# A planned attention and two-layer kernel on one core: new constants and a longer search for the plan's order

## The chip, the cores and the metric

The kernel runs on one core of one Trainium2 chip, in one launch. The time is the device time of one execution in microseconds (us). Smaller is better. Before the change three executions took 516.48, 516.94 and 519.18 us; their median is 516.94 us.

The engines are named as the profile names them: PE is TensorE, PEld its loading of weights, DVE is VectorE, ACT is ScalarE, POOL is GpSimd, SP is SyncE, which here only issues transfers.

## The reference

There are 4 sequences of 576 rows and 512 columns. Three layers follow one another; all arithmetic is asked for to the accuracy of 32-bit floats, and the weights come as 64-bit floats.

```python
# 1. attention: 8 heads of 64 columns; heads 0-3 see the last 32 positions,
#    heads 4-7 see earlier positions with the same remainder modulo 32
scores = scale * q @ k.T;  scores = where(mask, scores, -1e9)
x = softmax(scores) @ v
# 2. channel mix: x_prev is x moved down by one row
xk = mu_k * x + (1 - mu_k) * x_prev;  xr = mu_r * x + (1 - mu_r) * x_prev
x = sigmoid(xr @ w_r) * (relu(xk @ w_k) ** 2 @ w_v)      # 512 -> 1024 -> 512
# 3. gated layer: a convolution over three rows makes the gate
h = relu(x @ w_in)                                        # 512 -> 1024
out = (h * sigmoid(conv3(h, conv_w))) @ w_out             # 1024 -> 512
```

## The kernel before

Each 32-bit operand of a large product is split into a high and a low part, and a product is three matrix multiplications (high by high, low by high, high by low), of 288 or 512 columns each.

The work of the core has two stages, each with a plan of its own.

**First stage: attention and the channel mix.** Attention of a sequence is 8 units (4 pairs of heads, 2 halves each). A unit has scores on PE (`sc`, line 560), a mask and a row maximum on DVE (`masked`, line 576), exponentials on ACT (`exps`, line 581), a division on DVE (line 592), a transposition on PE (`tr`, lines 604 and 614) that ACT or DVE copies out (`pt`), the product with the values on PE (`pv`, lines 637 and 646), and a copy out into `xT`. The channel mix works on chunks of half a sequence (288 columns). `mix` makes `mx`, then its high and low parts: set `Y` for w_r, set `X` for w_k (lines 734 to 737; the high parts on ACT, the low parts on DVE). `Y00` to `Y31` and `X00` to `X31` are four blocks of 128 rows each, high (second digit 0) and low (second digit 1). Weights come in pieces: a transfer of the raw 64-bit words (`raw`), three instructions that make 32-bit words (`narrow`: `wb` at line 386, `wt` at 393, 394 and 397), and two that split them (`wrh` and `wrl`, `wkh` and `wkl`, `wvh` and `wvl`, lines 436 and 437). The products of the channel mix (`mm`) are all at line 755. For sequence 0 come 96 matmuls with w_r (eight groups of 12) and 192 with w_k, whose groups need all of `X`, then those with w_v. The other sequences follow; their attention is laid between the products.

**Second stage: the gated layer.** Products with w_in (`hh`, line 1010; 16 pairs of blocks of 42 matmuls each, four pairs to a sequence), a chain of DVE and ACT instructions for each of two blocks in a pair (`hb`, `c`, lines 1018 to 1059), its split (`gA`, `gB`, lines 1063 and 1064), and the products with w_out (`oo`, line 1078; 18 groups of 24 matmuls).

**What sets the order.** The code of the two stages adds jobs to a `Plan`: a job has its engines with a cost on each, a function that issues its instructions, what it reads and writes, and the number of bytes of a transfer. `Plan.run` goes through the jobs as if in time: it takes the job that can start earliest on its engine by the plan's costs (of those that start together the one with the highest rank), and puts it next on that engine. Jobs with two engines (mostly copies) go to the one that is earlier. The instructions are issued in exactly the order that comes out. The plan knows buffers (a `Space` has a tag and a number of buffers; a new one waits until an old one is released), the time of transfers (`DMA_RATE`, in bytes per us, `DMA_LATENCY`), the loading of a table on ACT (1.29 us where the table changes), and a model of how PE gets its instructions (`CHUNK`, `AHEAD`, `FETCH`, `CROWD`). Where PE would idle for longer than 0.48 us early in the first stage, the kernel puts matmuls without use on it (`stir`, line 922, from a tile of zeros named `idle`; 10 more stand at the start, into `scrap`): the number is the planned idle time less 0.3 us, divided by 0.17 us.

`search` repeats `run` with ranks changed at random by `vary`, from a list of seeds in `STEPS`: each seed changes the ranks that the seed before left. Only seeds that were kept when the list was made stand in it: 39 for the first stage and 30 for the second.

Of the kernel before, what the change touches and what calls it, by code (L numbers as in the profile page):

```python
# [2 lines left out]

# [24 lines left out]
BANKS = {"sc": 2, "tr": 2, "pv": 1, "mm": 3}  # L28
WARM, MIXES, BEHIND = 10, 2, (0, 3)
REBIAS = 2.0 ** -112  # L30
DMA_RATE, DMA_LATENCY = 280.0e3, 2.0
FOREVER = 1.0e9
PREFER, PREFER_FROM, BESIDE = 0.5, 20.0, 0.3
QUEUE, FEED = 64, 0.0142
CHUNK, AHEAD, FETCH, CROWD = 256, 85, 4.0, (0.3, 7.0)
GAP = {("mm", "half"): 0.09, ("tr", "half"): 0.17, ("tr", "tr"): 0.08}
ENTER = {("half", "mm"): 0.11, ("tr", "mm"): 0.085, ("half", "tr"): 0.05}
STEPS = (
    (
# [4 lines left out]
    ),  # L44
    (
# [3 lines left out]
    ),  # L49
)  # L50
HALF_ARRAY = {"sc", "pv"}
BLOCKS = ("B11", "B21", "B22", "T4", "T1", "T2", "T3")
WEIGHTS = ("A11", "A12", "A22", "S3", "S4", "S1", "S2")
# [4 lines left out]
SCRATCH = 1024  # L58
TAIL = 20.0
LQ, LK, LW, LB, LEAD = 64, 64, 96, (5, 4), 3  # L60
STIR_UNTIL = 60.0
BANKED = {"sc", "tr", "pv", "mm"}
RIGHT = {"raw", "ws", "wt", "wb", "qk", "vt", "pr", "nmx", "sums", "rec", "pt"}
LATENCY = {"PE": 0.22, "ACT": 0.16, "DVE": 0.12, "POOL": 0.12, "SP": 0.0}
# [27 lines left out]
class Plan:  # L92
# [89 lines left out]

    def vary(self, seed, keep, at, end):

        draw, tried = random.Random(seed), list(keep)
        t0, width = draw.uniform(0.0, end), draw.choice((8.0, 25.0, 400.0))
        amount, share = draw.choice((0.3, 1.0, 3.0)), draw.choice((0.05, 0.3))
        for i, j in enumerate(self.jobs):
            if abs(at[i] - t0) <= width / 2 and draw.random() < share:
                rank, lean = tried[i]  # L190
                if len(j.engines) > 1 and draw.random() < 0.5:
                    lean = draw.uniform(-0.6, 0.4)
                tried[i] = rank + draw.gauss(0.0, amount), lean
        return tried

    def search(self, start=None, steps=()):
# [26 lines left out]
    def run(self, start=None, limit=None):  # L223

        free = dict(start or dict.fromkeys(LATENCY, 0.0))
        dma, table, out, kind, filled, fetched, usable, leave = 0.0, None, [], "mm", 0.0, AHEAD, 0.0, 0.0
        wait = {j: len(j.before) for j in self.jobs}
        at = {j: [] for j in self.jobs}
        ready = {e: [] for e in LATENCY}
        left, todo = len(self.jobs), sum(j.engines.get("PE", 0.0) for j in self.jobs)  # L230

        def release(j):
            for e in j.engines:
                t = max([end + (ITSELF if by == e else LATENCY).get(by, 0.0) for end, by in at[j]], default=0.0)
                ready[e].append((t, j))

        for j in self.jobs:
            tags = {s.tag for s in j.spaces}
            j.kind = "half" if ("sc" in tags or "vt" in tags) else "tr" if "tr" in tags else "mm"
            if not wait[j]:  # L240
                release(j)
        while left:
            best, bound = None, FOREVER
            for e, jobs in ready.items():
                now = free[e]
                for t, j in jobs:
                    if t < now:
                        t = now
                    if t > bound + 1.0:
                        continue  # L250
                    for s in j.spaces:
                        if not s.open:
                            t = max(t, self.slot(s, j))
                    if t > bound + 1.0:
                        continue
                    late = t
                    if e == "DVE" and len(j.engines) > 1:
                        late += j.lean + PREFER * (t > PREFER_FROM)
                    if e == "PE":
                        late += max(0.0, self.feed(j, t, filled, fetched, usable, dma)[0] - t - j.engines[e])  # L260
                        late -= BESIDE * (kind == j.kind == "half")
                    key = (round(late, 2), -j.rank, j.n)
                    if t < FOREVER and (best is None or key < best[0]):
                        best, bound = (key, t, e, j), late
            assert best, "no job can start"
            _, t, e, j = best
            if e == "PE":
                t = max(t, free[e] + (GAP.get((kind, j.kind), 0.0) if kind != "half" else leave * (j.kind != "half")))
                idle = t - free[e]
                if self.stirred and 5.0 < t < STIR_UNTIL and idle > 0.48 and self.room(j, free[e]):  # L270
                    j.room, j.idle = self.room(j, free[e]), int((idle - 0.3) / 0.17)
                    fetched += 2 * j.idle
                    if fetched % CHUNK < 2 * j.idle:
                        usable = t + FETCH + CROWD[0] * min(CROWD[1], max(0.0, dma - t))
                else:
                    j.room = None
            for s in j.spaces:
                if not s.open:
                    s.open = True
                    self.opened[s.tag] += 1  # L280
            cost = j.engines[e]
            if e == "PE":
                cost += ENTER.get((kind, j.kind), 0.0)
                filled, fetched, usable = self.feed(j, t, filled, fetched, usable, dma)
                cost = max(cost, filled - t)
                kind, leave = j.kind, j.leave
                todo -= j.engines[e]
                if limit is not None and t + cost + todo > limit:
                    return None
            if j.table and j.table != table:  # L290
                cost += 1.29
                table = j.table
            if j.nbytes:
                free[e] = t + cost
                dma = max(dma, t + DMA_LATENCY) + j.nbytes / DMA_RATE
                j.end = dma
            else:
                free[e] = j.end = t + cost
            for k in j.engines:
                ready[k] = [x for x in ready[k] if x[1] is not j]  # L300
            for s in j.spaces:
                s.left -= 1
                s.end = max(s.end, j.end + LATENCY[e] * (not j.nbytes))
            for k in j.after:
                at[k].append((j.end, None if j.nbytes else e))
                wait[k] -= 1
                if not wait[k]:
                    release(k)
            out.append((j, e, t, j.end))
            j.done = True  # L310
            left -= 1
        return out
# [3 lines left out]
def block_kernel(ctx, tc, qkL, qkS, vL, vW, vS, mu_k, mu_r, w_k, w_v, w_r, w_in, conv_w, w_out, ident, mask_l, mask_w, mask_s, out):  # L316
# [603 lines left out]
    def stir(n, into, anew=True):  # L920
        for _ in range(n):
            pe.matmul(into[:, :T], idle[:, :P], idle, start=anew, stop=anew)
# [40 lines left out]
    def issue(stirred=False):  # L963
        plan.stirred = stirred
        with tc.manual_schedule():
            if stirred:
                stir(WARM, scrap)
            for job, e, start, end in plan.search(START if stirred else SECOND, STEPS[not stirred]):
                if e == "PE":
# [237 lines left out]
```

## Time and profile before

| | |
|---|---|
| three executions | 516.48, 516.94, 519.18 us |
| the profiled execution | 519.4 us, of which the trace's span is 517.6 us |
| PE busy | 508.3 us (98% of the span), 4886 matmuls |
| weight loads (PEld) busy | 472.0 us (91%) |
| DVE busy | 386.7 us (75%), 1142 instructions |
| ACT busy | 352.0 us (68%), 1075 instructions |
| DMA | 90.27 MB, mean 174 GB/s |
| chain that ended last, by engine | PE 85%, ACT 9%, DMA 3%, DVE 3%, issue 1% |
| granted clock of PE, mean | 0.998 |

All times in the views are us from the start of the span. A busy PE is not PE at work on the reference: the matmuls of `stir` count as busy too. Stages are found by the names: `mm` alone ends the first stage, and the first long run of `hh` begins the second.

### The profile page before, as it was taken

The numbers are of one execution on the slowest core, as the hardware profiler recorded it, in microseconds if no ns is written. First come the engines' busy times: TensorE is split into PE (matmuls) and PEld (weight loads), VectorE is DVE, ScalarE is ACT, GpSimd is POOL, SyncE is SP. The second block draws the span as 40 slices with busy tenths as digits, with TensorE's granted clock in tenths as the row PEclk, the third lists the DMA queues.
The fourth block names the chain that finished last, engine by engine and source line by source line (L and its number), as shares of the span: only waits on it lengthen the run. The fifth ranks groups of instructions, "written<-read, shape, count | busy, mean of one in ns | idle before, by whom it ended". The sixth has DMA issues, their size and how long they took to land.

```text
span 517.6 us, 12872 instructions
## 1 busy us (share of the span) xinstructions
PE 508.3 (98%) x4886; PEld 472.0 (91%) x4886; DVE 386.7 (75%) x1142; ACT 352.0 (68%) x1075; POOL 1.6 (0%) x15
## 2 busy tenths in 40 slices
PE   8989999999999999999999999999999999999997
PEld 5679999899999899999999999999998898988885
DVE  3999999898957988868877415699984697970910
ACT  5999996899758999857799243466663465542520
POOL 0000000000000000000000000000000000000000
PEclk9999999999999999999999999999999999999999
DMA  8956664884385982597683730854162163110111
GB/s 291 325 186 210 209 201 159 293 272 155 132 277 187 312 294 96 194 321 206 240 304 120 226 104 2 304 203 140 47 222 76 57 204 152 47 41 27 36 41 61
DMA packets 50653, 90.27 MB, mean 174 GB/s; under 512 B 4256, under 2 KB 32672, under 8 KB 50592
## 3 DMA queue, kind: packets, MB, share of 16 engines
q1 hardware_dynamic: 50304, 89.29, 51.5%
q8 instruction: 38, 0.62, 0.5%
q14 instruction: 23, 0.19, 0.1%
q10 hardware_dynamic: 288, 0.16, 0.1%
HBM read 60.80 MB, written 28.64 MB: 173 GB/s over the span
## 4 chain that ended last, share of the span: by engine, by line
PE 85%; ACT 9%; DMA 3%; DVE 3%; issue 1%; ACTq 0%; DVEq 0%
PE mm L755 43%; PE oo L1078 19%; PE hh L1010 17%; ACT pr L581 3%; PE sc L560 2%; PE pv L646 2%; PE tr L614 1%; DMA raw<-in_w_in 1%; ACT mx L734 1%; ACT wb L386 1%; DMA wi_d<-ws 1%; DMA qk<-in_qkL 1%; ACT Y L736 1%; DVE pr L576 1%; DVE pr L592 0%
## 5 line engine op out<-in xcount | busy, mean ns | idle before, releaser
L1010 PEld LDWEIGHTS hh<-x,wi 128*128 128x128 f32 x672 | 91.9, 188 | 2.1 <-DVE x L819 0.3
L1010 PE MATMUL hh<-x,wi 128*128 128x288 f32 x672 | 93.4, 296 | 0.1
L755 PE MATMUL mm<-X,wvh 128*128 128x288 f32 x448 | 83.9, 298 | 0.0
L755 PE MATMUL mm<-Y,wkh 128*128 128x288 f32 x384 | 68.1, 295 | 0.0
L755 PEld LDWEIGHTS mm<-X,wvh 128*128 128x128 f32 x448 | 66.9, 188 | 0.3
L581 ACT ACTIVATE pr<-pr,nmx 128x54 f32<-128x54 f32 (+2 forms) x160 | 53.8, 347 | 4.9 <-DVE nmx L576 4.8
L755 PEld LDWEIGHTS mm<-Y,wkh 128*128 128x128 f32 x384 | 56.4, 188 | 0.0
L755 PE MATMUL mm<-Y,wrh 128*128 128x288 f32 x256 | 56.0, 300 | 0.3 <-ACT rs L767 0.2
L1057 DVE SCALAR_TENSOR_TENSOR c<-hb,cw_sb,c 128x576 f32<-128x576 f32 x64 | 50.2, 812 | 0.4
L755 PE MATMUL mm<-X,wvl 128*128 128x288 f32 x224 | 47.9, 295 | 0.0
L755 PEld LDWEIGHTS mm<-Y,wrh 128*128 128x128 f32 x256 | 42.2, 188 | 1.5 <-ACT rs L767 0.4
L1078 PE MATMUL oo<-wo,gAh 128*128 128x512 f32 x160 | 43.2, 391 | 0.0
L755 PE MATMUL mm<-Y,wkl 128*128 128x288 f32 x192 | 40.9, 294 | 0.0
L755 PE MATMUL mm<-Y,wrl 128*128 128x288 f32 x128 | 38.1, 297 | 0.8 <-DVE wrl L437 0.7
L1088 ACT ACTIVATE ob<-oo 128x512 f32<-128x512 f32 x17 | 10.0, 597 | 38.5 <-PE oo L1078 38.1
L755 PEld LDWEIGHTS mm<-X,wvl 128*128 128x128 f32 x224 | 35.9, 188 | 0.0
L1078 PE MATMUL oo<-wo,gBh 128*128 128x512 f32 x128 | 34.4, 390 | 0.0
L1078 PEld LDWEIGHTS oo<-wo,gAh 128*128 128x128 f32 x160 | 29.1, 188 | 5.2
L1058 ACT ACTIVATE c<-c 128x576 f32<-128x576 f32 x32 | 21.8, 683 | 16.6 <-DVE c L1057 16.4
L581 ACT ACTIVATION_READ_ACCUMULATOR pr<-pr,nmx 128x1 f32 x160 | 32.2, 201 | 0.0
L778 ACT ACTIVATE rl<-mm 128x288 f32<-128x288 f32 x64 | 25.6, 406 | 9.3 <-PE mm L755 9.2
L796 DVE TENSOR_TENSOR X<-sq,X 128x288 fp32r<-128x288 f32 x48 | 21.7, 456 | 13.6 <-ACT X L794 11.8
(123 smaller groups left out, 1072.4 us busy)
## 6 DMA issues: line engine op xcount, KB each, us to landing
x_d<-xo SPq DMA_DIRECT2D x42, 288.0 KB, 3.0
x<-x_d SPq DMA_DIRECT2D x21, 576.0 KB, 4.7
wi_d<-ws SPq DMA_DIRECT2D x24, 256.0 KB, 3.4
wi<-wi_d SPq DMA_DIRECT2D x6, 896.0 KB, 6.2
qk<-in_qkS SPq DMA_DIRECT2D x8, 599.0 KB, 5.5
out<-ob SPq DMA_DIRECT2D x18, 256.0 KB, 2.0
qk<-in_qkL SPq DMA_DIRECT2D x7, 592.0 KB, 4.9
raw<-in_w_k SPq DMA_DIRECT2D x8, 512.0 KB, 3.9
```

What stands on the lines that cost most here:

```text
L386: act.activation(b(), hw, AF.Copy, scale=REBIAS)
L560: pe.matmul(bank_of[j]()[to + u:to + u + m, at_[j]:at_[j] + nk], qk()[r, qo[j] + u:qo[j] + u + m], qk()[r, ko[j] + u:ko[j] + u + nk], star ...
L581: act.activation(pr()[:, k], pr()[:, k], AF.Exp, bias=nmx()[:, i:i + 1], scale=-1.0, accum_out=sums()[:, i:i + 1])
L646: pe.matmul(outs_[odd]()[r, i * nq + u:i * nq + u + m], vt()[part, v, r], pt()[part, o:o + m], start=True, stop=True)
L755: pe.matmul(o(), w_cols(name, j, t, part), x_[t](), start=(t == 0 and part == 0 and x_ is xhi), stop=(t == nk - 1 and x_ is xlo))
L778: plan.add({"ACT": 0.295}, lambda e: act.activation(r(), o(), AF.Relu), [o], [r])
L796: plan.add({"DVE": 0.37}, lambda e: dve.tensor_tensor(l_(), sq(), h_().bitcast(F32), ALU.subtract), [sq, h_], [l_])
L1010: pe.matmul(o(), w(hw, j), x()[:, hx, j], start=anew and n == 0 and j == 0, stop=last and n == 2 and j == 1, skip_group_check=True)
L1057: plan.add({"DVE": 0.735}, lambda e, k=k: dve.scalar_tensor_tensor(c(), h()[:, k:k + S], cw_sb[:, k * NF + f:k * NF + f + 1], c(), ALU.mul ...
L1058: plan.add({"ACT": 0.6}, lambda e: act.activation(c(), c(), AF.Sigmoid), [c], [c], table="sigmoid")
L1078: pe.matmul(o(), x_()[:, f, col:col + P], wsp["wo", f]()[:, part], start=(f == 0 and x_ is th and part == 0), stop=(f == NF - 1 and x_ is tl))
L1088: act.activation(ob(), o(), AF.Copy, scale=0.5)
```

## The change

Three things change; the instructions of a job, its operands and its dependencies do not.

- Constants of the plan: `DMA_RATE` 280 to 365 (thousand bytes per us), `FETCH` 4.0 to 4.4 and `CROWD` (0.3, 7.0) to (0.4, 6.0) in the model of PE's instruction fetch; the plan starts with the exponential's table loaded instead of none; a PE job of the first stage that starts before 6.0 us counts 1.7 times; and an idle PE before 7.0 us gets one `stir` matmul for each 0.26 us instead of each 0.17 us.
- `vary` draws its numbers by its own arithmetic instead of the library's, and has a second kind of change: with a chance of 0.4 it shifts the ranks of 4 to 120 neighbouring jobs together.
- `STEPS` holds 61 seeds for the first stage and 43 for the second. The key of a job is rounded in another way.

```diff
-DMA_RATE, DMA_LATENCY = 280.0e3, 2.0
+DMA_RATE, DMA_LATENCY = 365.0e3, 2.0
-CHUNK, AHEAD, FETCH, CROWD = 256, 85, 4.0, (0.3, 7.0)
+CHUNK, AHEAD, FETCH, CROWD = 256, 85, 4.4, (0.4, 6.0)
-STEPS = (
+STEPS = ((20200000001, 20200000002, 20200000011, 20200000056, 20200000115, 20200000125, 20200000148, 20200000347, 20200000574, 20200000890,
...
-STIR_UNTIL = 60.0
+STIR_UNTIL, COLD = 60.0, 6.0
...
+        tried, early, whole = list(keep), draw() < 0.5, draw() < 0.4
+        if whole:
+            first = int(draw() * len(tried) * (0.4 if early else 1.0))
+            span, size = (4, 12, 40, 120)[int(draw() * 4.0)], (1.0, 4.0, 12.0)[int(draw() * 3.0)]
+            more = size * bell()
+            for i in range(first, min(first + span, len(tried))):
+                tried[i] = tried[i][0] + more, tried[i][1]
+            return tried
...
-        dma, table, out, kind, filled, fetched, usable, leave = 0.0, None, [], "mm", 0.0, AHEAD, 0.0, 0.0
+        dma, table, out, kind, filled, fetched, usable, leave = 0.0, "exp", [], "mm", 0.0, AHEAD, 0.0, 0.0
...
-                    key = (round(late, 2), -j.rank, j.n)
+                    key = (int(late * 100.0 + 0.5), -j.rank, j.n)
...
-                    j.room, j.idle = self.room(j, free[e]), int((idle - 0.3) / 0.17)
+                    j.room, j.idle = self.room(j, free[e]), int((idle - 0.3) / (0.26 if t < COLD + 1.0 else 0.17))
...
-                cost += ENTER.get((kind, j.kind), 0.0)
+                cost = cost * (1.0 + 0.7 * (self.stirred and t < COLD)) + ENTER.get((kind, j.kind), 0.0)
```

The new order differs on every engine. PE has the same products, scores and transpositions, and 45 `stir` matmuls instead of 54. ACT and DVE exchange a few jobs that can go to either. Three places follow. Line numbers of the new kernel are higher by 20 (`sc` is at line 580 there, `stir` at 942).

The first is PE just after the 10 matmuls at the start. `sc_150` is the first part of the scores of the first unit, `sc_166` (new: `sc_159`) the second, and `sc_183` and `sc_188` (new: `sc_180` and `sc_183`) are those of the second unit. Before:

```order
L560 MATMUL sc_150<-qk_131 64x96 x6
L922 LDWEIGHTS idle_116
L922 MATMUL sc_166<-idle_116 128x288
L922 LDWEIGHTS idle_116
L922 MATMUL sc_166<-idle_116 128x288
L922 LDWEIGHTS idle_116
L922 MATMUL sc_166<-idle_116 128x288
L922 LDWEIGHTS idle_116
L922 MATMUL sc_166<-idle_116 128x288
L560 MATMUL sc_166<-qk_131 64x96 x4
```

After:

```order
L580 MATMUL sc_150<-qk_132 64x96 x6
L580 MATMUL sc_159<-qk_132 64x96 x4
L942 LDWEIGHTS idle_116
L942 MATMUL mm_178<-idle_116 128x288
L580 MATMUL sc_180<-qk_132 64x96 x2
L580 MATMUL sc_183<-qk_132 64x96 x2
```

The four matmuls without use between the two parts of the first unit are gone, and of the two behind the second part one is left.

The second is ACT before the last block of `X` (high part, `X30`) of sequence 0. `rs` are the results of the w_r groups, `wb` and `wkh` belong to the weights, and `pr_808` are exponentials of sequence 1. Before:

```order
L767 ACTIVATE rs_821<-mm_823 128x288
L581 ACTIVATE pr_808,sums_882<-pr_808,nmx_809 128x64 x3
L734 ACTIVATE mx_898<-xT0_134,muk_sb_80 128x576
L436 ACTIVATE wrh3_907<-wt_864 128x512
L386 ACTIVATE wb_918<-raw_813 128x512
L734 ACTIVATE mx_922<-xT0_134,muk_sb_80 128x576
L767 ACTIVATE rs_818<-mm_867 128x288
L767 ACTIVATE rs_821<-mm_893 128x288
L436 ACTIVATE wkh0_939<-wt_912 128x512
L581 ACTIVATE pr_808,sums_882<-pr_808,nmx_809 128x64 x2
L736 ACTIVATE X20_104<-mx_898 128x576
L736 ACTIVATE X30_106<-mx_922 128x576
```

After:

```order
L787 ACTIVATE rs_803<-mm_806 128x288
L756 ACTIVATE X10_102<-mx_814 128x576
L406 ACTIVATE wb_847<-raw_746 128x512
L787 ACTIVATE rs_801<-mm_828 128x288
L754 ACTIVATE mx_860<-xT0_134,muk_sb_80 128x576
L754 ACTIVATE mx_869<-xT0_134,muk_sb_80 128x576
L456 ACTIVATE wkh0_878<-wt_816 128x512
L787 ACTIVATE rs_803<-mm_849 128x288
L406 ACTIVATE wb_888<-raw_796 128x512
L756 ACTIVATE X20_104<-mx_860 128x576
L756 ACTIVATE X30_106<-mx_869 128x576
```

The exponentials of sequence 1 (`pr_808`) are no longer here. Counted from the start of ACT's order, 14 exponentials of sequence 1 stood ahead of `X30` before and 3 do now. On DVE, 16 masks of sequence 1 stood ahead of `X31` and 9 do now, and one division of sequence 1 (128x320) is gone from there. On PE, 16 score matmuls and 3 transpositions of sequence 1 stood ahead of the 120th matmul of the channel mix before and stand behind it now (the trace shows each score matmul as two).

The third is PE in the second stage, at the last `hh` (the matmuls with w_in). Before, the last `hh` and the first rows of what follows:

```order
L1010 MATMUL hh_7211<-x2_3_6847,wi32_5301 128x288 x6
L1078 MATMUL oo_7253<-wo0_5656,gAh_5821 128x512
L1078 MATMUL oo_7253<-wo1_5658,gAh_5821 128x512
L1078 MATMUL oo_7253<-wo0_5656,gAh_5821 128x512
L1078 MATMUL oo_7253<-wo1_5658,gAh_5821 128x512
```

After:

```order
L1030 MATMUL hh_6871<-x2_2_6685,wi34_5317 128x288 x6
L1030 MATMUL hh_6905<-x2_3_6725,wi32_5292 128x288 x6
L1098 MATMUL oo_7153<-wo0_5647,gAh_5819 128x512
L1098 MATMUL oo_7153<-wo1_5671,gAh_5819 128x512
L1098 MATMUL oo_7153<-wo0_5647,gAh_5819 128x512
```

Behind the last `hh` stood 120 `oo` matmuls before; now 192 stand there. The `hh` are issued earlier, the `oo` later.

## Rows read from the trace of the kernel before

**Rows 1.** Busy by stretch: length, PE, PEld, DVE, ACT, POOL, PEclk, DMA share, GB/s.

```profile
10.00:20.00 10.00, 9.73 (x187) 7.09 (x184) 9.59 (x75) 9.18 (x45) 0.00 (x0) 1.00 1.04 356
...
30.00:40.00 10.00, 9.12 (x124) 7.71 (x125) 9.46 (x29) 10.00 (x32) 0.00 (x0) 1.00 0.63 209
40.00:50.00 10.00, 9.73 (x100) 9.09 (x78) 9.96 (x23) 10.00 (x31) 0.00 (x0) 1.00 0.63 197
...
327.60:514.00 186.40, 186.25 (x1087) 168.19 (x1087) 128.90 (x232) 91.03 (x192) 0.00 (x0) 1.00 0.32 111
```

**Rows 2.** The chain that ended last: start in us, us, what stands in it.

```profile
41.08 1.00 ACT pr L581 x6
...
47.22 0.79 ACT wb L386
48.35 2.65 PE mm L755 x18
51.01 0.50 PE sc L560 x24
52.19 36.81 PE mm L755 x276
...
100.65 0.94 issue
...
486.58 27.34 PE oo L1078 x120
```

**Rows 3.** Timeline, 0 to 12 us: start, us, instruction, in brackets idle time before it.

```profile
0.73 1.34 SPq L365 DMA_DIRECT2D qk<-in_qkL  x3
...
4.94 1.14 PE L922 MATMUL sc<-idle 128*128 128x288 bf16 x4
...
6.01 0.90 PE L560 MATMUL sc<-qk 64*64 64x96 f32 x8
...
6.96 0.26 DVE L576 CUSTOM_DVE_ANT_0 pr<-sc,mw_sb 128x96 f32<-128x96 f32 x1 [1.28 <-PE sc L560]
...
7.27 0.38 ACT L581 ACTIVATE pr<-pr,nmx 128x96 f32<-128x96 f32 x1 [0.73 <-DVE nmx L576]
...
8.14 0.26 DVE L576 CUSTOM_DVE_ANT_0 pr<-sc,mw_sb 128x96 f32<-128x96 f32 x1 [0.73 <-PE sc L560]
...
9.62 0.26 DVE L576 CUSTOM_DVE_ANT_0 pr<-sc,mw_sb 128x96 f32<-128x96 f32 x1 [0.68 <-PE sc L560]
```

**Rows 4.** Transfers by issue: KB each, median us from issue to landing.

```profile
qk<-in_qkL SPq DMA_DIRECT2D x1, 384.0 KB, 3.9
```

**Rows 5.** Groups on DVE, 0 to 52 us: count, busy us, mean ns, idle before.

```profile
L576 DVE CUSTOM_DVE_ANT_0 pr<-sc,ml_sb 128x64 f32<-128x64 f32 x18 | 3.1, 217 | 0.0
...
L592 DVE TENSOR_TENSOR pr<-pr,rec 128x320 f32<-128x320 f32 x1 | 0.5, 492 | 0.0
```

**Rows 6.** Timeline of PE, 30 to 41 us.

```profile
33.76 0.52 PE L614 MATMUL tr<-id_sb,pr 128*128 128x128 f32 x3
34.11 0.41 PE L922 MATMUL mm<-idle 128*128 128x288 bf16 x2
...
39.77 0.45 PE L560 MATMUL sc<-qk 64*32 64x64 f32 x32
40.15 0.40 PE L755 MATMUL mm<-Y,wrh 128*128 128x288 f32 x1
```

**Rows 7.** Waits: who waited for whom, us in total, times, longest.

```profile
DVE wt L393 <- DMA raw<-in_w_k: 1.0, 1, 1.0
```

**Rows 8.** Busy by stretch, 334 to 395 us: all engines, columns as in rows 1.

```profile
334.00:395.00 61.00, 61.00 (x400) 57.48 (x399) 58.05 (x105) 39.74 (x85) 0.00 (x0) 1.00 0.48 161
```

**Rows 9.** The same stretch, DVE's line 1059 alone (one instruction to a block).

```profile
334.00:395.00 61.00, 11.05 (x15) 1.00 0.48 161
```

**Rows 10.** Groups on PE, 0 to 12 us: count, busy us, mean ns, idle before.

```profile
L922 PE MATMUL scrap<-idle 128*128 128x288 bf16 x10 | 2.6, 445 | 1.1 <-POOL xT L690 1.1
...
L922 PE MATMUL mm<-idle 128*128 128x288 bf16 x9 | 1.4, 288 | 0.0
```

More of the change, by code (lines that the diff above doesn't have):

```diff
@@ L1 @@
-import random
 from contextlib import ExitStack
@@ L34 @@
 QUEUE, FEED = 64, 0.0142
-CHUNK, AHEAD, FETCH, CROWD = 256, 85, 4.0, (0.3, 7.0)
+CHUNK, AHEAD, FETCH, CROWD = 256, 85, 4.4, (0.4, 6.0)
 GAP = {("mm", "half"): 0.09, ("tr", "half"): 0.17, ("tr", "tr"): 0.08}
 ENTER = {("half", "mm"): 0.11, ("tr", "mm"): 0.085, ("half", "tr"): 0.05}
-STEPS = (
-    (
[4 rows of a table removed]
-    ),
-    (
[3 rows of a table removed]
-    ),
-)
+STEPS = ((20200000001, 20200000002, 20200000011, 20200000056, 20200000115, 20200000125, 20200000148, 20200000347, 20200000574, 20200000890,
[11 rows of a table added]
 HALF_ARRAY = {"sc", "pv"}
@@ L183, in vary, with draw, bell @@
     def vary(self, seed, keep, at, end):
-        draw, tried = random.Random(seed), list(keep)
-        t0, width = draw.uniform(0.0, end), draw.choice((8.0, 25.0, 400.0))
-        amount, share = draw.choice((0.3, 1.0, 3.0)), draw.choice((0.05, 0.3))
+        state = seed
+        def draw():
+            nonlocal state
+            state = (state + 0x9E3779B97F4A7C15) % 2 ** 64
+            x = (state ^ state >> 30) * 0xBF58476D1CE4E5B9 % 2 ** 64
+            x = (x ^ x >> 27) * 0x94D049BB133111EB % 2 ** 64
+            return ((x ^ x >> 31) >> 11) / 2.0 ** 53
+        def bell():
+            x = 0.0
+            for _ in range(12):
+                x += draw()
+            return x - 6.0
+        tried, early, whole = list(keep), draw() < 0.5, draw() < 0.4
[6 more added lines that the diff above has]
+            return tried
+        t0, width = draw() * (min(end, 110.0) if early else end), (8.0, 25.0, 400.0)[int(draw() * 3.0)]
+        amount, share = (0.3, 1.0, 3.0)[int(draw() * 3.0)], (0.05, 0.3)[int(draw() * 2.0)]
         for i, j in enumerate(self.jobs):
-            if abs(at[i] - t0) <= width / 2 and draw.random() < share:
+            if abs(at[i] - t0) <= width / 2 and draw() < share:
                 rank, lean = tried[i]
-                if len(j.engines) > 1 and draw.random() < 0.5:
-                    lean = draw.uniform(-0.6, 0.4)
-                tried[i] = rank + draw.gauss(0.0, amount), lean
+                if len(j.engines) > 1 and draw() < 0.5:
+                    lean = draw() - 0.6
+                tried[i] = rank + amount * bell(), lean
         return tried
```

18 rows, old and new, of the table STEPS are left out of this document.

## The prediction

> **What bounds the kernel now.** I read the stretches first, then the chain, then the timeline where the chain changes engine. From 52 us on PE is the bound: in the second stage it is busy for 186.25 of 186.40 us [rows 1], and the chain there is one run of PE after another. All instructions that serve the reference stay, so PE's work can't shrink; an order can only take away time in which PE stands or does useless work. Nearly all of that lies before 52 us. There the chain lies on ACT: ACT is busy for 10.00 of 10 us from 30 to 40 and from 40 to 50, DVE for 9.46 and 9.96 [rows 1], and the last piece of ACT in the chain, a weight's `wb` at 47.22, is followed by products on PE from 48.35 on [rows 2]. What PE waits for there is the last block of `X`: `X30` on ACT, then `X31` on DVE. The reader is to see two things: who is full (ACT and DVE until 48 us, PE after 52), and that an instruction moved from before `X31` to behind it costs nothing on ACT or DVE later, but may cost PE.
>
> **The start, load on ACT and DVE.** Ahead of `X30` ACT has 11 exponentials of sequence 1 fewer (14 before, 3 now). Three of them with their accumulator reads take 1.00 us in the chain [rows 2], so 11 take 3.67. One `wb` comes in, 0.79 us by its row [rows 2]; the copies that change engines about cancel. ACT: -2.9 us. Ahead of `X31` DVE has 7 masks fewer, 3.1 us for 18 [rows 5], so 1.2 us, and one division fewer, 0.49 [rows 5]: -1.7 us; other copies that left DVE might bring 0.5 more. Both engines are needed for `X31`, and DVE gains less, so I take -1.7 for when it is ready.
>
> **The start, the first microseconds.** The second part of the first unit's scores starts at 6.01, behind four matmuls without use that take 1.14 us [rows 3]. Its data come with the second of three transfers issued from 0.73 on in 1.34 us, so at about 1.2, and land 3.9 us later [rows 3, 4]: 5.1. The new order has nothing in between, so this part can start 0.9 us earlier. DVE idled 1.28 us for it, then 0.73 and 0.68 us for the next scores, 2.69 together, and ACT 0.73 us [rows 3]. Of the 1.28 I take 0.9, of the other two half (0.7), because the new order also puts sums, which wait for ACT, ahead of DVE's masks: -1.6 us, between 0 and -2.7. So `X31` is ready 3.3 us earlier, and PE's wait ends at 48.35 - 3.3 = 45.05.
>
> **The start, on PE.** At the end of its wait PE had 20 products left of the first 120 (2.65 us, from 48.35 to 51.01 [rows 2]). In the new order only 12 of the 120 need the last blocks of `X` and everything else can run before: 96 products with w_r and 12 with the first two blocks. I find no wait on DVE for these: `wrl3` and `wkl0` stand well ahead of `X31`. So 8 products fewer lie behind the wait, 8 x 0.133 us (36.81 us for 276 [rows 2]) = 1.06 us more. Against this PE owes the 16 scores (0.38 us, 39.77 to 40.15) and 3 transpositions (0.35 us, 33.76 to 34.11) that it had done by then and now does while it is the bound [rows 6]: +0.73. Sum of the start: -1.7 - 1.6 - 1.06 + 0.73 = **-3.6 us**. Bounds: -1.0 (no idle time saved, no products moved ahead) and -5.2 (all 2.69 us saved, 0.5 more on DVE).
>
> **Transfers.** The plan now counts 365 thousand bytes per us; 10 to 20 us moved 356 GB/s with the engines full [rows 1], so this is what the trace has, where 280 was cautious. A plan that trusts the higher rate may ask for a raw weight too early: DVE waited once for one, 1.0 us [rows 7]. 0 to +1.0; I take 0, because DVE is by then ahead of PE, which needs 3.2 us (24 x 0.133) for each w_k piece.
>
> **Instruction fetch.** The chain has one stretch in which PE waited for nothing that the profile shows, 0.94 us at 100.65 [rows 2]. `FETCH` and `CROWD` move jobs around such stretches. I take 0, between -0.94 and +0.94. The Trainium skill (Runtime: NRT & Kernel Launch, section Instruction fetch mechanics) says that the sequencer loads its instructions a block ahead and that crossing a block is mostly hidden. By that page the two constants describe nothing and this term is 0 on both sides; the row has 0.94 us that no engine explains, so the trace doesn't fully agree.
>
> **Middle of the first stage.** From the 120th product to the second stage PE turns from products to attention 31 times before and 29 times after, counted in the order. Two turns fewer, each below the 0.35 us of three transpositions [rows 6]: 0 to -0.7. I take 0. The 9 `stir` matmuls fewer fill waits and are worth nothing by themselves.
>
> **Second stage.** The last `hh` stood 120 `oo` before the end, 27.34 us [rows 2]; now 192, so 192 x 0.228 = 43.7 us. Every `hh` has to be fed by DVE up to 16 us earlier, and DVE's 128.90 us of work [rows 1] begin no earlier relative to it. DVE handled 15 blocks in 61.00 us, 4.07 us each, busy 58.05 of them [rows 8, 9]. I compare PE's work ahead of pair p in the stage (0.132 us for each `hh`, 0.228 for each `oo` ahead in the order) with DVE's for the blocks of the pairs before the last one, (2p - 2) x 4.07. Before, the difference falls to -0.8 us at pair 4 and then grows to 24, and PE never stood; so -0.8 is harmless. After, it falls to -1.7 at pair 8 and stays between -1.0 and +4 until pair 15. That is 0.9 us below what the trace has shown to be harmless, at one pair. I take **+0.5 us**, between 0 and +4 (the rival below).
>
> **Sum.** -3.6 + 0.5 = -3.1 us. The profiled execution took 519.4 us (span 517.6), which becomes 516.3; the median of the runs shown is 516.94, 2.5 us lower, and I set the same difference against it: **513.8 us**.
>
> **Rival 1: the start hardly moves (516.4 us).** The idle time at the front turns into waits for ACT's sums, and PE's products with w_r end later than I count, so that only the load goes: -1.7 + 0.73 + 0.5 = -0.5. For it: ACT and DVE are full from 30 us on either way, and what ACT gives up early it has to do later. Against it: the 1.14 us of useless matmuls stood between data that had landed and DVE that waited.
>
> **Rival 2: DVE becomes the bound of the second stage (517.3 us).** DVE idled 2.95 of 61.00 us in its fullest stretch [rows 8], mostly for ACT. The new order has it full without a lead until pair 15, 113 us into the stage, so 113/61 x 2.95 = 5.5 us of such pauses, of which a plan with a little margin passes on some 4: -3.6 + 4 = +0.4. Against it: PE hid the same pauses completely before 395 us.
>
> **Rival 3: the clock rises later; slower (520.8 us).** A matmul without use takes 445 ns in the first 10 and 288 ns soon after [rows 10]; the listed stretches all show a granted clock of 1.00, the 2.4 GHz level, so the start must lie at the other level, 1.2 GHz. With four useless matmuls gone after 5 us, the rise could come later, say 10 us later. PE was busy 9.73 us from 10 to 20 [rows 1]; at 445/288 that is 0.55 x 9.73 = 5.3 us more, and the 1.6 us at the front go too: -3.1 + 5.3 + 1.6 = +3.8. It decides once PE is as full as from 10 to 20 and still at the lower level. Against it: 35 `stir` matmuls stay behind the first 10, and scores come in place of those removed. The Trainium skill (TensorE: Matmul & The Clock Gate, Part 1) says that the lower clock is the default, that activity lifts it and that idleness brings it back; by that rule useless work removed early is a risk, and the trace agrees so far that the first matmuls are slow.
>
> **Numbers.** Half a percent, 2.6 us, is about what a measurement of this kernel tells from no change. Forecast 0.60 (own range 511.3 to 515.6), rival 1 0.23, rival 2 0.11, rival 3 0.06. Faster means below 514.4: three quarters of the forecast, 0.46, and 0.04 of the rivals' lower ends: 0.50. Slower means above 519.5: rival 3 and the upper ends of rivals 1 and 2, 0.12. Same: 0.38. The range 511.0 to 517.9 takes in the sum's bounds at the start (-5.2 with +0.5 would be 512.2, and 1.2 for the turns and the fetch) and rivals 1 and 2, and leaves out rival 3.
>
> **What would show it.** In the changed kernel the first long run of products should begin about 4 us before 48; DVE's first idle time behind the first scores should be below 0.5 us; the run of `hh` should begin near 324; and PE should be busy for all but 1 us of the second stage. It is wrong if the second stage begins later than 326.5 (the start), if PE stands in the second stage with DVE as releaser (rival 2), or if matmuls without use still take 440 ns after 8 us (rival 3).

## The result and the profile after

The changed kernel is slower: 523.96 us (median of six executions, 522.92 to 525.96) against 519.27 us for the kernel before beside it on the same chip (six, 516.48 to 520.05); ratio 1.0105, 95% interval 1.008 to 1.013, so 5.4 us with 4.2 to 6.8 (the two medians alone differ by 4.7). The profiled execution took 525.96 us (span 524.1); it is the slowest of the six.

The stretches of the changed kernel, columns as in [rows 1]; the last one is its second stage:

```profile
10.00:20.00 10.00, 6.92 (x127) 4.94 (x126) 6.39 (x47) 7.25 (x36) 0.00 (x0) 1.00 0.92 296
20.00:30.00 10.00, 9.82 (x214) 7.33 (x209) 9.81 (x59) 9.56 (x45) 0.00 (x0) 0.83 0.87 301
30.00:40.00 10.00, 9.46 (x143) 7.68 (x141) 10.00 (x28) 9.95 (x29) 0.00 (x0) 1.00 0.69 234
40.00:50.00 10.00, 10.00 (x78) 10.00 (x77) 10.00 (x25) 10.00 (x24) 0.00 (x0) 1.00 0.46 155
333.80:520.40 186.60, 186.45 (x1087) 168.06 (x1087) 129.57 (x234) 90.48 (x189) 0.00 (x0) 1.00 0.32 111
```

The second stage is as before (186.45 busy of 186.60 us, where [rows 1] have 186.25 of 186.40); it only begins 6 us later. From 10 to 20 us PE, DVE and ACT stand for about a third of the time, where before they were nearly full. Pieces of its chain (start, us, what), with every transfer in it, to be held against [rows 2]:

```profile
3.06 9.00 DMA vt<-in_vW
12.09 6.22 DMA raw<-in_w_r
37.91 1.00 ACT pr L601 x6
39.26 39.24 PE mm L775 x294
...
142.25 4.05 DMA wi_d<-ws
149.83 6.65 DMA raw<-in_w_in
161.84 1.06 ACT pr L601 x6
172.62 7.69 DMA wi_d<-ws
186.62 4.17 DMA x_d<-xo
192.13 6.61 DMA x_d<-xo
219.91 3.59 DMA x_d<-xo
225.15 3.83 DMA wo_d<-ws
...
476.72 43.72 PE oo L1098 x192
```

Transfers make up 10% of the chain (3% before). From 142 us on, all but one of them are stores of `xo` and `ws` to DRAM, whose data nobody needs soon. One case shows how a store reaches PE. ACT's and PE's timelines at the store that is issued at 192.13 and lands 6.61 us later:

```profile
196.92 0.39 ACT L787 ACTIVATE rs<-mm 128x288 f32<-128x288 f32 x1
198.75 0.44 ACT L842 ACTIVATE xo<-rs 128x288 fp32r<-128x288 f32 x1 [1.44 <-DMA x_d<-xo]
...
200.53 0.39 ACT L787 ACTIVATE rs<-mm 128x288 f32<-128x288 f32 x1
```

```profile
199.04 0.42 PE L775 MATMUL mm<-Y,wkh 128*128 128x288 f32 x2
200.96 0.53 PE L775 MATMUL mm<-Y,wkh 128*128 128x288 f32 x2 [1.50 <-ACT rs L787]
```

ACT wants to write `xo`, of which there are two buffers, and stands until the store of one has landed; behind it in ACT's queue stands the tanh (`rs`) that empties the product bank PE wants next; PE waits 1.50 us. From 80 to 280 us PE was busy 198.62 of 200 us before (the first line) and 195.46 now (the others: length, PE busy, granted clock, DMA share, GB/s):

```profile
sum 200.00, PE 198.62; mean PE 39.72
```

```profile
160.00:200.00 40.00, 37.82 (x591) 1.00 0.77 253
200.00:240.00 40.00, 38.41 (x370) 1.00 0.66 226
240.00:280.00 40.00, 40.00 (x516) 1.00 0.52 174
sum 200.00, PE 195.46; mean PE 39.09
```

Waits for transfers from 80 to 275 us (who waited for what: us in total, times, longest). Those of ACT and DVE add up to 24.6 us here, 15.8 of them for stores; the same sums are 9.2 and 4.7 in the kernel before. The changed kernel, then the kernel before:

```profile
ACT xo L842 <- DMA x_d<-xo: 9.6, 12, 1.7
...
ACT wb L406 <- DMA raw<-in_w_in: 3.6, 3, 2.3
...
DVE ws L471 <- DMA wo_d<-ws: 3.5, 2, 2.9
...
ACT wb L406 <- DMA raw<-in_w_out: 2.7, 3, 1.9
```

```profile
ACT wb L386 <- DMA raw<-in_w_in: 4.3, 4, 2.0
DVE ws L451 <- DMA wi_d<-ws: 2.4, 2, 1.3
ACT xo L822 <- DMA x_d<-xo: 2.3, 1, 2.3
```

The transfers themselves did not get slower as a whole. Three kinds of them (KB, median us from issue to landing, the changed kernel; before they took 3.0, 5.5 and 4.9):

```profile
x_d<-xo SPq DMA_DIRECT2D x42, 288.0 KB, 3.4
...
qk<-in_qkS SPq DMA_DIRECT2D x8, 599.0 KB, 5.5
...
raw<-in_w_in SPq DMA_DIRECT2D x8, 512.0 KB, 4.3
```

Of the ten kinds that carry `qkS`, raw weights of products or halves, five took longer than before, four shorter and one as long; the largest rises, 1.6 us each, are those of w_r's raw weights and of the stores to `wo_d`. What changed for all is the plan's picture of them. For the same jobs its medians were 4.0 (`xo`) and 8.6 us (`qkS`) with 280, and are 2.9 and 4.5 with 365: the old plan had them later than they came, the new one has them sooner.

The start. DVE's and PE's timelines at 14 to 20 us:

```profile
15.63 0.16 DVE L614 TENSOR_SCALAR sums<-sums 128x4 f32<-128x4 f32 x1
18.33 0.46 DVE L413 TENSOR_SCALAR wt<-raw 128x512 uint16<-128x512 uint16 x1 [2.54 <-DMA raw<-in_w_r]
...
19.10 0.52 DVE L393 COPY pt<-tr 96x384 f32<-96x384 f32 x1
```

```profile
16.87 0.65 PE L942 MATMUL mm<-idle 128*128 128x288 bf16 x4
19.72 0.47 PE L657 MATMUL pv<-pt,vt 96*64 96x64 f32 x9 [2.20 <-ACT wb L406]
```

The new order has the conversion of the first raw weight (`wt`) so early in DVE's queue that DVE stands 2.54 us in front of it, and PE then 2.20. The profile puts PE's wait down to ACT's `wb`, which was done at 19.01; PE starts at 19.72, right after DVE's copy `pt`, which `pv` reads and which stands behind the conversion.

For all runs I worked out one curve from the matmul records: the moment at which PE has done so many us of work (each kind of matmul at its usual duration in the trace, the useless ones at 0), minus that work. "Start" is the time lost so when 36 us of work are done (at 58 to 65 us), "middle" what is lost from there to 280 us of work (end of the first stage). "Plan" is when the plan has PE finish the first stage, "`hh`" when the second stage begins in the trace. e1 to e17 are the experiments of the next section.

| kernel | rate in the plan | plan | `hh` | start | middle | ratio to before |
|---|---|---|---|---|---|---|
| before | 280 | 321.2 | 325.1 | 25.1 | 9.9 | 1 |
| changed | 365 | 318.4 | 331.3 | 25.1 | 16.1 | 1.0105 |
| e1 | 365 | 318.4 | 325.7 | 21.8 | 13.8 | 1.0087 |
| e3 / e4 | mixed | | 325.3 / 331.2 | 25.0 / 24.0 | 10.2 / 17.2 | 1.0027 / 1.0101 |
| e5 | 365 | 318.4 | 324.7 | 23.5 | 11.1 | 1.0038 |
| e6 | mixed | | 324.3 | 22.5 | 11.7 | 1.0010 |
| e7 | 280 | 321.0 | 321.9 | 24.1 | 7.7 | 0.9996 |
| e8 | 280 | 320.8 | 323.2 | 22.5 | 10.6 | 1.0027 |
| e9 | 335, latency 2.8 | 319.7 | 324.5 | 23.8 | 9.9 | 0.9990 |
| e10 | 280 | | 323.5 | 24.4 | 9.0 | 0.9989 |
| e14 | 365 | 319.8 | 333.6 | 24.6 | 18.1 | 1.0227 |
| e15 | 365 | 319.3 | 338.5 | 29.2 | 19.2 | 1.0231 |
| e16 | 280 | 321.0 | 324.7 | 24.6 | 9.3 | 1.0038 |
| e17 | 335, latency 2.8 | 320.6 | 325.2 | 23.8 | 10.6 | 1.0012 |

Start, middle and `hh` are of one execution each, and not always of a typical one: the profiled execution is the slowest of six for the changed kernel and for e15, the fastest of ten for e1 (519.97 us, median 522.55) and the second fastest of twelve for e7 and e8. The ratios are over 6 to 12 executions against 23 to 35 of before on the same chip (six for the changed kernel) and need not equal the quotient of two medians. One slow execution each of e1 and e8 is left out of the ratio.

### The profile page after: what moved, and what is told of

It reads as the page before. It is cut to its first block, busy times and chain, and to the rows that moved or that the text cites. A ratio compares the mean times of both kernels' runs of the same rounds, so it can differ in the third digit from the quotient of the medians.

```text
span 524.1 us, 12853 instructions
## 1 busy us (share of the span) xinstructions
PE 508.9 (97%) x4877; PEld 472.4 (90%) x4877; DVE 386.4 (74%) x1142; ACT 353.0 (67%) x1075; POOL 1.1 (0%) x15
## 4 chain that ended last, share of the span: by engine, by line
PE 70%; DMA 10%; ACT 9%; DVE 8%; issue 2%; SPq 0%; DVEq 0%; ACTq 0%
PE mm L775 31%; PE oo L1098 19%; PE hh L1030 15%; DMA x_d<-xo 3%; DMA wi_d<-ws 2%; DMA vt<-in_vW 2%; PE sc L580 2%; ACT mx L754 1%; ACT X L814 1%; ACT rl L798 1%; DMA raw<-in_w_in 1%; PE pv L666 1%; ACT pr L601 1%; PE tr L634 1%; DMA raw<-in_w_r 1%
## 5 line engine op out<-in xcount | busy, mean ns | idle before, releaser
L775 PE MATMUL mm<-Y,wkh 128*128 128x288 f32 x384 | 70.0, 297 | 2.3 <-ACT rs L787 1.5
L1078 ACT ACTIVATE c<-c 128x576 f32<-128x576 f32 x32 | 21.9, 685 | 19.2 <-DVE c L1077 18.7
L775 PEld LDWEIGHTS mm<-Y,wkl 128*128 128x128 f32 x192 | 30.6, 188 | 0.0
```

Of the source, the lines that this page charges most:

```text
L775: pe.matmul(o(), w_cols(name, j, t, part), x_[t](), start=(t == 0 and part == 0 and x_ is xhi), stop=(t == nk - 1 and x_ is xlo))
L1078: plan.add({"ACT": 0.6}, lambda e: act.activation(c(), c(), AF.Sigmoid), [c], [c], table="sigmoid")
```

## The experiments

Every kernel below but e5 has the second stage in the order of before. Orders are written out as tables, so that pieces of two orders can be joined and single jobs moved; the instructions stay the same. The diffs of `ORDERS` below say in words what the table holds, and those of the plan's constants are of the planner that made the table. Of the loop that issues the jobs this leaves (shortened):

```diff
-            for job, e, start, end in plan.search(START if stirred else SECOND, STEPS[not stirred]):
+            for n, e, *stirs in ORDERS[not stirred]:
...
-                job.emit(e)
+                jobs[n].emit(e)
```

**Where the loss lies: e1, e3, e4.**

```diff
-ORDERS = (changed first stage, changed second stage)
+ORDERS = (changed first stage, second stage of before)                                     # e1
+ORDERS = (changed up to 78 us of plan, then before, second stage of before)               # e3
+ORDERS = (before up to 78 us of plan, then changed, second stage of before)               # e4
```

> The first stage in the new order, the second stage in the order of before. Theory A (the loss sits in the first stage, where ACT and DVE now stand in front of transfers that land later than the plan has them): about 5.5 to 6 of the 7 us by which the two profiled executions differ come before the second stage begins, so this kernel takes some 523.5 us, at most 1 us less than the changed kernel, and 4 to 4.5 more than the kernel before. Rival R (the second stage's order: DVE becomes its bound): 519 to 520, as before.

> The new order up to its plan's 78 us (transfers, exponentials, scores, first products), everything left in the order of before, the second stage too. Theory A: the start neither gains nor loses much, since its gain of 3.6 us that I forecast is eaten by the first raw w_r weight, which is issued later (12.1 instead of 9.8 us) and makes DVE wait 2.5 us: 518 to 520, within 1 us of before. Rival C (the start gains its 3.6 us, only the profiled execution had late transfers): 515.7. Rival D (the loss is made at the start, by a clock that falls): 523.

> The order of before up to its plan's 78 us, everything left of the first stage in the new order, the second stage as before. Theory A (loss between about 150 and 262 us): about 523.5 us, 4 to 5 us over before. Rival D (loss made at the start): 519, as before.

Measured: e1 522.55 us, 1.0087 (1.0061 to 1.0113); e3 519.84, 1.0027 (1.0010 to 1.0045); e4 523.43, 1.0101 (1.0077 to 1.0126); before 518.45. The loss is in the first stage behind its start, as e4 shows by itself; e1, at 522.55, came out a little lower than I had put it. The new start alone doesn't gain its 3.6 us, it loses 1.4 (0.5 to 2.3), where I had put it within 1 us of before. Rivals R, C and D fall.

**What stands in the middle: e5.** The order on every engine is the changed kernel's; only what the stores of `ws` (shown) and of `xo` (likewise) read is another tile, so that `xo` and `ws` are free at once. The kernel leaves out the real stores: what lands in DRAM is not the halves. SP no longer waits for the data of a store either, so the transfers behind a store can go out sooner; e5 frees both at once.

```diff
-        dma(lambda i=i: dst(i), lambda x=x: x()[:, :n].bitcast(F32), P * n * 4, [x], ...
+        dma(lambda i=i: dst(i), lambda: wsp["wk", 0][0]()[:, :n].bitcast(F32), P * n * 4, [wsp["wk", 0][0]], ...
```

> The changed kernel's order on every engine, word for word, but the stores of the x2, w_in and w_out halves to DRAM read a weight tile that nobody rewrites (wk's first) instead of xo and ws, as many bytes in rows as long: xo and ws need not wait for a store, and SP's stores not for their data. What is stored is then not the halves. Theory A (ACT and DVE wait for stores: ACT's xo 11.6 us in 14 places): most of the loss in the middle goes, 518.5 to 520.5 us. Rival B (the middle's loss is in how the jobs are ordered and split between ACT and DVE, whatever the transfers do): 523 to 524, as the changed kernel.

Measured: 520.74 us, 1.0038 (1.0021 to 1.0055), against 1.0105 for the changed kernel: 3.5 us of its 5.4 go with the stores' waits (2 to 5 by the two intervals). The time is a little above what I had put. The middle loses 11.1 instead of 16.1 us. The waits for stores from 80 to 275 us, 15.8 us in the changed kernel, are gone; those of ACT and DVE for loads rose from 8.8 to 14.9, so the gain doesn't come from loads that land sooner. The largest of them (us in total, times, longest):

```profile
ACT wb L406 <- DMA raw<-in_w_out: 7.6, 3, 5.0
```

So waits for stores are shown to cost a large part of the loss, by the middle value most of it; that the rest is waits for raw weights was only read from this line.

**The number that does it: e7, e9.**

```diff
-DMA_RATE, DMA_LATENCY = 365.0e3, 2.0
+DMA_RATE, DMA_LATENCY = 280.0e3, 2.0      # e7
+DMA_RATE, DMA_LATENCY = 335.0e3, 2.8      # e9
```

> The changed kernel's planner and final ranks with one number put back, the transfers' rate (280 in place of 365 KB per us), and from there 15,000 more tries of the same search; second stage in the order of before. Its plan ends 2.5 us later than the changed kernel's (320.96 against 318.42 us for PE). Theory A (the higher rate makes the plan put ACT and DVE in front of transfers too early): faster than the changed first stage (e1, 522.55) by 3 to 5 us, 517.5 to 519.5, and few ACT waits for xo's stores. Rival B (order and split of the jobs cost the time, whatever the transfers' rate in the plan): 521.5 to 523, as e1. Rival P (the plan's own end decides): 525, 2.5 over e1.

> As e7, but the transfers' numbers fitted to what the traces of both kernels show without a reserve: rate 335 KB per us, 2.8 us of latency; 15,000 tries from the changed kernel's ranks; PE's planned end 319.68 us; second stage as before. Theory A: between the changed first stage and e7, 519 to 521, since half of the transfers then land as planned and half later. Rival B: 521.5 to 523.

Measured: e7 517.83 us, 0.9996 (0.9981 to 1.0010); e9 517.73, 0.9990 (0.9974 to 1.0006); before 517.92. Both were searched anew from the changed kernel's final ranks. Against e1 (1.0087) e7 is 0.9%, 4.7 us, faster, though its plan ends 2.5 us later. Rivals B and P fall. e9 I had put too high: it needs no reserve beyond landing times that are right. In e7's profile, one of its fastest executions, PE never stands from 80 to 280 us, and the waits for transfers there add up to 7.4 us:

```profile
sum 200.00, PE 200.00; mean PE 40.00
```

```profile
ACT wb L406 <- DMA raw<-in_w_in: 2.7, 3, 1.1
...
DVE ws L471 <- DMA wo_d<-ws: 1.0, 1, 1.0
ACT xo L842 <- DMA x_d<-xo: 1.0, 2, 0.6
```

**The rate alone, and the luck of the search: e8, e14 to e17.** e8, e14 and e17 have all the old numbers but for the rate, in e17 the latency too (e8: none changed), and start from the final ranks of before; e15 and e16 have all the new numbers but for the rate (e15: none changed) and start from there too.

```diff
-DMA_RATE, DMA_LATENCY = 280.0e3, 2.0
+DMA_RATE, DMA_LATENCY = 365.0e3, 2.0      # e14; e15 beside the other new numbers
+DMA_RATE, DMA_LATENCY = 335.0e3, 2.8      # e17
```

> The planner of before with all its old numbers, from its final ranks, but with 15,000 more tries of the new search moves (four were kept; PE's planned end 321.22 to 320.83 us); second stage as before. This is the longer search alone. Theory A (the search is harmless where the numbers keep a reserve): 518 to 519, within 1 us of before. Rival S (a search that goes on picks orders that lean on the plan's errors): 520 to 522.

> The planner of before with all its old numbers but one, the transfers' rate (365 for 280 KB per us), from its final ranks with 15,000 tries; PE's planned end 319.79 us; second stage as before. Its partner is e8, the same with 280 (planned 320.83, measured 519.55). Theory A (the rate alone makes the loss): 2 to 5 us over e8, 521.5 to 524. Rival L (e1 and e7 differ by the luck of the order that each search happened to keep): 518 to 520, as e8.

> All the new numbers (365), but searched from the final ranks of before instead of the changed kernel's: another order for the same numbers, PE's planned end 319.26 us; second stage as before. Theory A: 2 to 5 us over its partner e16, 520.5 to 523. Rival L: within 1 us of e16.

> As e15 with the rate 280, PE's planned end 320.99 us. Theory A: 517 to 518.5, as e7. Rival L: within 1 us of e15.

> The planner of before with the transfers' numbers as fitted to the traces (335 KB per us, 2.8 us latency) and all else old; PE's planned end 320.55 us; second stage as before. Theory A, as e9 (517.73): 517 to 518.5. Rival (e9's time came from its other new numbers): 519 to 520.5.

Measured: e8 519.55 us, 1.0027 (0.9997 to 1.0057); e14 529.44, 1.0227 (1.0188 to 1.0267); e15 530.54, 1.0231 (1.0204 to 1.0258); e16 519.65, 1.0038 (1.0022 to 1.0054); e17 519.02, 1.0012 (0.9993 to 1.0031). e14 against e8 and e15 against e16 give 2.0 and 1.9%, 10 us, for the rate, twice the upper end of what I expected; in the profile of e15 4.6 us of it lie at the start (29.2 against 24.6). Rival L falls: at 365 all three orders are slower, the changed kernel's being the mildest, and at 280 or 335 none of the five is more than 0.4% over before. The longer search by itself neither gains nor clearly loses (e8, between what theory A and rival S had). e16 and e17 came out up to 1.2 us above theory A; e17 lies at the lower edge of its rival, and its interval tells it neither from e9 nor from before. e14's PE from 80 to 280 us, and what its ACT and DVE wait for most (80 to 275 us):

```profile
sum 200.00, PE 194.17; mean PE 38.83
```

```profile
DVE ws L471 <- DMA wi_d<-ws: 6.9, 3, 4.2
ACT ws L470 <- DMA wo_d<-ws: 6.1, 1, 6.1
ACT wb L406 <- DMA raw<-in_w_in: 5.1, 3, 3.0
```

**The start: e6, e11 to e13.** e6 moves the first raw weight's conversion; the others load 576 KB for nothing ahead of the fourth transfer (e11 in the order of before, e12 in e3's, e13 in e6's).

```diff
-ORDERS = (e3's first stage, ...)
+ORDERS = (e3's with wt, wb, wrh0 of the first raw weight and mur1, muk1 moved back on DVE and ACT, ...)    # e6, e13
...
                 jobs[n].emit(e)
+                for i in range(2 * (stirred and n == 42)):                                                 # e11 to e13
+                    nc.sync.dma_start(out=plan.tags["mx"][i](), in_=qkS[1, 0, :, S * i:S * (i + 1)])
```

> As e3 (the new order up to its plan's 78 us, the rest and the second stage as before), but the first raw w_r weight's conversion stands about 5 us of plan later in DVE's and ACT's queues, and mur's and muk's small jobs a few places later on DVE; nothing else is moved. Theory A (DVE stands 2.5 us in front of that weight when the first transfers land late, PE then stands 2.1 us and its clock falls for some us; the order of before has the conversion later and loses nothing): 517 to 518.5 us, 1.5 to 3 us under e3's 519.84, and no wait over 0.5 us of DVE for the raw weight. Rival E (the new start loses elsewhere, the conversion's place is not it, or moving it starves the products behind it): 519.5 to 521, as e3.

> The kernel before with two more loads of 288 KB each, of no use, put between the third and the fourth transfer of SP's queue, so that everything behind them (the first raw weight too) is issued and lands some 2 us later in every execution. Theory A (the old order has the raw weight's conversion late enough): at most 1 us slower than before, 517.5 to 519. Rival E (a late start costs every order the same): 520 to 521, 2 to 3 us slower.

> As e3 (new order up to 78 us, the rest as before), with the same two useless loads as in e11. Theory A (the new order has DVE stand in front of the first raw weight, PE behind it, and the clock falls): 2.5 to 4 us over e11, 521 to 523. Rival E: as e11 plus the 1.4 us between e3 and before, 519 to 521.

> As e6 (as e3, but the first raw weight's conversion and mur's and muk's small jobs later on DVE and ACT), with the same two useless loads. Theory A (that conversion's place is what makes the new start weak against late transfers): 2 us or more under e12, 518.5 to 520. Rival E: as e12.

Measured: e6 518.68 us, 1.0010 (0.9992 to 1.0028); e11 519.62, 1.0013 (0.9998 to 1.0028); e12 519.41, 1.0024 (1.0004 to 1.0043); e13 519.06, 1.0008 (0.9991 to 1.0025). My theory of the start, that late transfers cost the new order 2.5 to 4 us more than the old one, falls: with two loads added to both, e12 and e11 are alike. The lateness was not quite the same, though: in the profiled executions the first raw weight landed at 21.13 us in e11 and at 18.13 in e12, about where it landed in e3 without the loads (18.08). Moving the conversion back gives 0.17% without and 0.16% with the extra loads; the intervals overlap, so it isn't shown.

What the traces do show is narrower. In e1, with the same start order as the changed kernel, the fourth transfer landed at 8.23 us (10.61 in the changed kernel), the raw weight at 15.11 (18.30), and DVE waited 0.88 us for it:

```profile
15.13 0.47 DVE L413 TENSOR_SCALAR wt<-raw 128x512 uint16<-128x512 uint16 x1 [0.88 <-DMA raw<-in_w_r]
```

In e4, which starts in the old order, that weight landed at 17.53 and nobody waited, since the conversion stands far behind:

```profile
21.61 0.16 DVE L614 TENSOR_SCALAR sums<-sums 128x6 f32<-128x6 f32 x1
21.68 0.45 DVE L413 TENSOR_SCALAR wt<-raw 128x512 uint16<-128x512 uint16 x1
```

Of the fourteen profiles in which the first qkS load is the fourth transfer and nothing was added, it landed at 8.2 to 8.8 us in five and at 10.2 to 11.8 in nine, whatever the order. The old start loses 25.1 and 24.4 us with early transfers and 24.0 with late ones; the new start 21.8 with early ones (e1) and 23.5, 25.0 and 25.1 with late ones. The gain that I forecast was seen only with early transfers, and in one execution (e1). That it hangs on them is read from these few profiles and not shown; why transfers come late in some executions stays open.

**Joined: e10.**

```diff
+ORDERS = (before up to 68 us of plan, then e7, second stage of before)
```

> The order of before up to its plan's 68 us, the rest of the first stage in e7's order (rate 280, searched anew), second stage as before. In e7's profiled execution the stretch from 60 us of PE work to the second stage lost 7.1 us, against 9.9 in before's, yet the times were equal. Theory A (e7's start is no better than the old one, its middle is): 516 to 517.3 us, 0.2 to 0.4% under before. Rival (what one execution of e7 showed in the middle is scatter): 517.5 to 518.5.

Measured: 518.29 us against 518.80, 0.9989 (0.9975 to 1.0004). The rival holds: what one execution of e7 showed in the middle doesn't come back in the time. No gain can be told, and no version here is measurably faster than the kernel before.

## Why the prediction was wrong

From the forecast of -3.1 us to the measured +5.4 it is 8.5 us: some 3.6 are a gain at the start that didn't come; the rest, about 5, is lost in the middle of the first stage.

- **Transfers, taken as 0 with bounds 0 to +1.0: the step that failed.** It read 356 GB/s from 10 to 20 us as proof of the rate 365. That is what the 16 engines moved together while they were full (share 1.04 in that row); a plan in which queues stand still needs the moment when one transfer lands. I put the plan's own rule (each transfer starts when the one before it is done, 2.0 us after its issue at the soonest) on the real issue times of the first stage from 80 to 290 us: with 365 the transfers of the two kernels land on average 0.55 (before) and 0.74 us (changed) later than it says, half of them by over 0.5 us; with 280 they land 1.0 us sooner, and 5 to 8% are late by over 0.5 us. The bound of 1.0 us was the single wait of [rows 7], in an order that had been made with a reserve; it says nothing of an order made without. Nor was it the only wait: the list that it comes from has DVE wait twice more, for w_v (0.9 us), and ACT for raw weights of w_in (4.3) and for stores of `xo` (5.6, of which 2.3 from 80 to 275 us, above). And I asked only whether DVE is ahead of PE for w_k's pieces; the waits came mostly on ACT (18.6 of 24.6 us), and mostly for buffers whose stores had not landed. Measured in place of 0: +3.9 us (e1) and +6.2 us (changed) in the middle of the profiled executions, 3.5 by e5 for the stores alone, 4.7 by e7 for the rate.
- **Start, -3.6.** Where the first transfers landed as early as in the execution that it was read from, the gain was there, in one execution: e1 loses 3.3 us less than before did. The profiled executions of before and of the changed kernel had both done 28 us of PE's work at 53.1 us, so the gain was 0 in that pair, and e3 gives +1.4 (0.5 to 2.3). What the forecast left out is again a transfer: it took the landing times of one execution as fixed. The second part of the first unit's scores began at 5.49, right behind its data, which landed at 5.44 and not at 5.1: 0.5 us gained and not 0.9. DVE idled 0.75 and 0.60 us where I wanted less than 0.5. The sign I had named for it misled: the long run of products begins at 39.26 instead of 52.19, but with more work left behind it. The other sign, a second stage that begins after 326.5, came (331.3), but what delayed it was the middle.
- **Middle of the first stage, 0 to -0.7.** Counting turns said nothing; the middle lost 16.1 us where it had lost 9.9, and by e5 most of that in waits that no count in the order shows.
- **Instruction fetch, 0.** Inside the bounds: the stretch of 0.94 us is gone, and the one of 0.76 us that the changed kernel's chain has at 80.95 stands before an instruction that waits for a semaphore (the one of 0.71 at 19.01 is the wait for `pt` above). But that the two constants describe nothing doesn't hold. In ten of the eighteen profiles PE stood for 0.3 to 1.0 us before an instruction that waits for nothing, twelve times in all (in e14 at 19.94, 31.97 and 107.90 us), and each time 193 or 194 instructions past a multiple of 256, with all PE instructions of the trace counted: the period of the plan's `CHUNK`.
- **Second stage, +0.5.** Right in the two profiles: from the first `hh` to PE's last matmul 189.2 us against 188.8. Rival 2 did not come.
- **Rival 1** had the start right, not its reason. **Rival 3** had the sign, not the mechanism: the useless matmuls run at full speed by then, as in [rows 10] (count; busy, mean ns; idle before):

```profile
L942 PE MATMUL mm<-idle 128*128 128x288 bf16 x9 | 1.6, 289 | 0.0
```

  The clock did fall, later: the granted clock is 0.83 from 20 to 30 us, so for a part of it at the 1.2 GHz level, behind a stretch in which PE was busy for 6.92 of 10 us, and 0.51 in e15, behind 5.91. With 0.17 of 10 us gone, that is at most 1.7 us of the changed kernel's start, an estimate. The Trainium skill (TensorE: Matmul & The Clock Gate, Part 1) says that idleness brings the lower clock back; the traces agree.

The changed kernel's loads of 512 KB, issued by SP beside others, took a median of 3.5 to 6.6 us. The Trainium skill (DMA: Bandwidth & Descriptors, section Anatomy of one DMA) gives a fit of 2.0 us and bytes over 436 GB/s, measured on the path of GpSimd; for 512 KB that would be an estimate of 3.2 us. A plan by the page's figure would be more hopeful still than the one with 365.

## What to carry to other kernels

In a static order with in-order queues the errors of a plan are not symmetric: a transfer that lands before its planned time costs little, one that lands after it stops its engine and whatever is queued behind. Here the rate that puts landings 1.0 us too late on average cost 0 to 0.4% (e7, e8, e16), the one that puts them 0.55 to 0.74 us too early 0.9 to 2.3% (e1, e14, e15). So give the planner landing times as the trace has them under load (here 335 KB per us and 2.8 us, or simply 280), not the highest throughput of a stretch, and compare the plan's end with the trace's: at 365 the plan promised 1.4 to 2.8 us, and the second stage began 7 to 19 us after the planned end of the first, at 280 or 335 1 to 5 us after it. Before pricing a stall that "DVE is ahead of", look at the buffers that wait for a store and at what stands behind that instruction in its queue.

## What was not expected of the hardware

The same first transfers, issued at the same times, land 2 to 3 us apart from one profile to the next (the fourth, 599 KB issued at 2.11 us, at 8.2 to 8.8 or at 10.2 to 11.8 us), also where the program is the same up to there: 8.23 us in e1 and 10.61 in the changed kernel, 8.17 in before and 11.16 in e4. And stores of 288 KB with a median of 3.4 us took up to 8.6 us (11.2 in the kernel before) when they were issued while three to five other transfers were under way.
